# Attention with memory slots and a SwiGLU block: another order of the loads in each round, and of the first gate and value products

## The chip, the cores and the metric

The kernel runs on one core of a Trainium2 chip. The metric is device time in microseconds (us) for one execution of the whole program; lower is better. The engines are TensorE (PE, with its weight loads shown apart as PEld), VectorE (DVE), ScalarE (ACT), GpSimd (POOL) and SyncE (SP). Each engine runs its own instructions in order and waits for the others, and for transfers, through semaphores.

## The reference

```python
def _attn_ref(q, k, v, phi):            # q, k, v: [8, 8, 576, 64]; phi: [8, 8, 576, 32]
    a = np.exp(phi - max over m);  a = a / sum over m
    k_m = einsum('bhsm,bhsd->bhmd', a, k)       # 32 memory slots for each head
    v_m = einsum('bhsm,bhsd->bhmd', a, v)
    scores = q @ k_m.T / sqrt(64)
    attn = softmax over the 32 slots of scores
    return attn @ v_m

def _moe_ref(x, w_gate, w_val, w_out):  # x: [4608, 512]; 512 -> 1536 -> 512
    g = x @ w_gate
    return (g * sigmoid(g) * (x @ w_val)) @ w_out
```

The attention's output, with its heads put side by side, is `x` of the second function: 8 batches of 576 tokens with 512 features. All inputs and the output are float32; the kernel computes its products in bfloat16.

## The kernel before, in words

All 8 batches run through the same stages, on 96 partitions of 6 tokens where tokens are the contraction.

*Memory sums.* `phi_exp` (line 146) exponentiates phi. `kv_sum` (line 160) multiplies it into keys and values, 48 small matmuls for a batch, and `kv_denominators` (line 172) makes the sums that `k_norm` and `v_norm` divide by. `kv_T` transposes the result (lines 210, 214) and copies it into `t_kT` (line 216). For batches 2 to 7 `kv_items` does keys and values together, so line 160 waits for both loads. For batches 0 and 1 keys (`k_items`) and values (`v_items`) go apart.

*Queries.* For batches 0 and 1 TensorE transposes them (`q_T`). For batches 2 to 7 a DMA transpose issued on SP does it (`load_qT`, line 99: from the tile `t_q` to `t_qT`).

*Scores.* `scores` (line 287) multiplies the transposed keys with the transposed queries, `z_inv` (line 307) makes the softmax denominators, `norm` (line 316) the weights `t_A`.

*Gate and value.* The values of the memory are first multiplied into the weights: `u_round` (line 330) makes `t_U` from `t_kT` and a chunk of 512 columns of both weight matrices, three chunks a batch; `u_item` does a whole chunk, `u_both_halves` one half of it. Each of 24 slots of a batch (`gv_slot`, line 364) then multiplies `t_U` with `t_A` for gate and value. ACT applies Silu (line 380), DVE multiplies (line 387). Slots 0 to 3 need only the first half of chunk 0, slots 4 to 7 its second half, slots 8 to 15 chunk 1.

*Output.* For each pair of batches 9 tiles of 128 tokens take 12 matmuls each (line 420). A tile is copied out of PSUM (lines 430, 432) and stored by SP (line 434). These units are kept in a list, the backlog, and put between other work.

*The order of the work* is written out by hand, and each engine follows it as written. A prelude issues the loads for batches 0 to 3 and the weights; then comes the hand-written start for batches 0 and 1; then a loop with one round for each batch from 2 to 7. A round takes the scores, softmax and slots of batch `b` and, spread between the slots, the memory sums of batch `b + 1` and its transposed queries. It also issues the loads for later batches: keys and values of `b + 1`, phi and queries of `b + 2`.

*The load queue.* All loads but the first two of phi are issued by POOL, one after the other. An issue waits until its buffer is free, and what follows waits behind it. Keys and values have two buffers in turn, phi two, `t_qT` two. The query tile has two slots, given out by hand:

```python
Q_SLOT = (0, 1, 0, 0, 1, 0, 1, 0)
```

Batches 2, 3, 5 and 7 share slot 0 and batches 4 and 6 share slot 1, where batch 1 was before. So the load of batch 3's queries waits for batch 2's DMA transpose, that of batch 5 for batch 3's, that of batch 6 for batch 4's, that of batch 7 for batch 5's; that of batch 4 waits for nothing that is still running. SP issues the DMA transposes and the stores, in order too; the transpose for batch 3 stands in the middle of its round (`n = 12` of 24), the later ones at the head of the slots.

Of the kernel before, what the change touches and what calls it, by code (L numbers as in the profile page):

```python
# [14 lines left out]
def kernel(  # L15
# [21 lines left out]
    B, H, S, D = q.shape  # L37
# [34 lines left out]
    def load_k(b):  # L72
        t = inp.tile([P, 2, H, J * D], BF16, tag="kv", name="t_kv")
        nc.gpsimd.dma_start(out=t[:, 0], in_=k[b].rearrange("h (p j) d -> p h (j d)", p=P))  # L74
        kvs[b] = t

    def load_v(b):
        nc.gpsimd.dma_start(
            out=kvs[b][:, 1], in_=v[b].rearrange("h (p j) d -> p h (j d)", p=P)
        )  # L80
# [10 lines left out]
    def load_q(b):  # L91
        t = inp.tile([P, H, J * D], BF16, tag=f"q{Q_SLOT[b]}", bufs=1, name="t_q")
        nc.gpsimd.dma_start(out=t, in_=q[b].rearrange("h (p j) d -> p h (j d)", p=P))  # L93
        qs[b] = t

    def load_qT(b):

        t = att.tile([128, H, 3, P], BF16, tag="qT", name="t_qT")
        nc.sync.dma_start_transpose(
            out=t.rearrange("p h j t -> p (h j) t"),  # L100
            in_=qs[b].rearrange("p h f -> p (h f)"),
        )
        for i in range(NP):
            qTs[b, i] = t[:, 2 * i:2 * i + 2].rearrange("p h j t -> p h (j t)")
# [5 lines left out]
    def load_w(which, c, half):  # L110

        src = (moe_w_gate, moe_w_val)[which]
        if half == 0:
            W[which, c] = wpool.tile(
                [128, 2, NP, HC], BF16, tag=f"W{which}{c}", name=f"W{which}{c}"
            )
        f0 = c * CH + half * HC
        nc.gpsimd.dma_start(
            out=W[which, c][:, half],
            in_=src[:, f0:f0 + HC].rearrange("(i p) f -> p i f", p=128),  # L120
        )
# [20 lines left out]
    def phi_exp(b):  # L142
        t = att.tile([P, J, NG, NP, M], BF16, tag="ephi", name="t_ephi")
        src = phis.pop(b).rearrange("p (i g) (j m) -> p g i j m", g=NG, m=M)
        for g in range(NG):
            nc.scalar.activation(  # L146
                out=t[:, :, g].rearrange("p j i m -> p i j m"), in_=src[:, g], func=AF.Exp
            )
        ephis[b] = t
# [84 lines left out]
    def k_items(b):  # L234


        def sums():
            box["k"] = ps.tile([128, NG * D + NG], FP32, tag="b", name="p_kv")
            kv_sum(b, box["k"], (0,))

        def norm():
            kv_denominators(b, box["k"], NG * D)
            k_norm(b, box["k"][:, 0:NG * D].rearrange("p (g a d) -> p g a d", g=NG, a=1))

        return [sums, norm, lambda: kv_T(b, (0,))]

    def v_items(b):


        def sums():  # L250
            p = ps.tile([128, NG * D], FP32, tag="b", name="p_kv")
            kv_sum(b, p, (1,))
            v_norm(b, p.rearrange("p (g d) -> p g d", g=NG))

        return [sums, lambda: kv_T(b, (1,))]
# [22 lines left out]
    def gv_banks():  # L278
        return [
            ps.tile([128, CH], FP32, tag="b", name=f"p_{'gv'[r]}") for r in range(2)  # L280
        ]

    def scores(b, g):
        p = gv_banks()
        for i in range(NP):
            for r in range(2):
                nc.tensor.matmul(  # L287
                    p[r][32 * i:32 * i + 32, 0:HALF],
                    lhsT=kTs[b][64 * r:64 * r + 64, g, 32 * i:32 * i + 32],
                    rhs=qTs[b, i][64 * r:64 * r + 64, g],  # L290
                    start=True,
                    stop=True,
                    tile_position=(64 * r, 32 * i),
                )
        e = att.tile([128, 2, HALF], BF16, tag=f"E{g}", name="t_E")
        for r in range(2):
            nc.scalar.activation(out=e[:, r], in_=p[r][:, 0:HALF], func=AF.Exp, scale=sm_scale)  # L297
        es[b, g] = e
# [23 lines left out]
    def u_round(b, parts, evac):  # L322

        banks = []
        for which, c, halves in parts:
            f0, f1 = HC * halves[0], HC * (halves[-1] + 1)
            p = [ps.tile([128, CH], FP32, tag="b", name=f"p_u{g}") for g in range(NG)]
            for i in range(NP):
                for g in range(NG):
                    nc.tensor.matmul(  # L330
                        p[g][32 * i:32 * i + 32, f0:f1],
                        lhsT=kTs[b][64 * g:64 * g + 64, 2, 32 * i:32 * i + 32],
                        rhs=W[which, c][64 * g:64 * g + 64, halves[0]:halves[-1] + 1, i],
                        start=True,
                        stop=True,
                        tile_position=(64 * g, 32 * i),
                    )
            for g in range(NG):
                if (b, which, c, g) not in Us:
                    Us[b, which, c, g] = upool.tile(  # L340
                        [128, CH], BF16, tag=f"U{which}{c}{g}", name="t_U"
                    )
                banks.append((Us[b, which, c, g][:, f0:f1], p[g][:, f0:f1]))
        for (t, p), e in zip(banks, evac):
            if e == "a":
                nc.scalar.copy(out=t, in_=p)  # L346
            else:
                nc.vector.tensor_copy(out=t, in_=p)  # L348
# [105 lines left out]
    def u_item(b, c, evac="avav"):  # L454

        both = ((0, c, (0, 1)), (1, c, (0, 1)))
        return lambda: u_round(b, both, evac)

    def u_both_halves(b, c, half, evac="avav"):

        both = ((0, c, (half,)), (1, c, (half,)))
        return lambda: u_round(b, both, evac)
# [4 lines left out]
    def run(items):  # L467
        for x in items:
            x()
# [10 lines left out]
    def exp_tables():  # L480
        nc.scalar.preload_act_table_set("natural_log_exp_and_others")  # L481

    def gv_slots(b):
        return [lambda s=s: gv_slot(b, s) for s in range(2 * NJF)]

    def warm(n):

        p = po.tile([128, DM], FP32, tag="o", name="p_oo")
        for _ in range(n):
            nc.tensor.matmul(p[:, 0:128], lhsT=bones, rhs=bones, start=True, stop=True)  # L490
# [15 lines left out]
    load_v(0)  # L506
    for which in range(2):
        load_w(which, 0, 0)
    for which in range(2):
        load_w(which, 0, 1)  # L510
    load_v(1)
    for c in range(1, NCH):
        for half in range(2):
            for which in range(2):
# [17 lines left out]
    k0, k1, v0, v1 = k_items(0), k_items(1), v_items(0), v_items(1)  # L532
# [35 lines left out]
    g0, g1 = gv_slots(0), gv_slots(1)  # L568
    warm(6)
    run([u_both_halves(0, 0, 0)])  # L570
    warm(6)
    run(g0[:2])
    run([u_both_halves(0, 0, 1)] + g0[2:5] + v1[:1] + g0[5:6] + v1[1:] + g0[6:7])
    run([u_item(1, 0)] + g0[7:8] + g1[:6])
    for c in range(1, NCH):
        s = 8 * c
        run([u_item(0, c)] + g1[s - 2:s] + g0[s:s + 4])
# [5 lines left out]
    def take(n):  # L583
        nonlocal backlog
        n = max(0, min(n, len(backlog)))
        part, backlog = backlog[:n], backlog[n:]
        return part

    for b in range(2, B):
        last = b + 1 == B  # L590
        exp_tables()
        if b == 2:
            load_qT(2)
            phi_exp(2)
            run(take(28))
            run(kv_items(2)[:1] + take(6) + kv_items(2)[1:] + take(14))
        run(take(2))
        for g in range(NG):
            scores(b, g)
        if not last:  # L600
            load_k(b + 1)
            load_v(b + 1)
        if b + 2 < B:
            load_phi(b + 2, nc.gpsimd)
            load_q(b + 2)
        run(take(8))
        if not last:
            phi_exp(b + 1)
        for g in range(NG):
            z_inv(b, g)  # L610
        nc.scalar.preload_act_table_set("silu_and_others")
        run(take(14))
        norm(b, 0)
        norm(b, 1)
        if b == 2:
            run(take(4))
            run([u_item(2, 0)] + take(6) + [u_item(2, 1)])
        run(take(12))
        rest = take(len(backlog))
        g = gv_slots(b)  # L620
        streams = [(g, 0, 24), (rest, 0, 24), ([u_item(b, 2)], 5, 6)]
        if not last:
            n = 12 if b == 2 else 0
            streams += [
                ([lambda: load_qT(b + 1)], n, n),
                (kv_items(b + 1), 8, 14),
                ([u_item(b + 1, 0)], 15, 17),
                ([u_item(b + 1, 1)], 21, 23),
            ]
        spread(*streams)  # L630
        flush_mul()
        backlog += out_list(b)
# [29 lines left out]
```

## Time and profile before

| | before |
|---|---|
| time, median of 3 runs | 261.36 us (260.73 to 262.14) |
| the profiled execution: time | 263.36 us |
| the profiled execution: span | 261.4 us |
| mean granted TensorE clock over the span | 0.987 |
| PE busy | 245.3 us |
| DVE / ACT / POOL busy | 153.2 / 167.0 / 36.3 us |
| HBM read / written | 42.47 MB / 9.44 MB |
| DMA transposes on SP | 6 |

The span runs from the first to the last instruction in the profile; the time of an execution has some 2 us around it. A timeline row has the start, the duration, the engine, the line of the kernel, the operation, output and inputs, the shape, and in brackets the idle time of the engine just before with what ended it. A row of the DMA view has output and input, the issuing queue, the number of issues, the size, and the time from issue to landing. Names such as `t_kv<-in_v_dram` read "into the tile t_kv from the input v".

### The profile page before, as it was taken

Reading aid. Unit: us, or ns where it says so; the run is one execution under the profiler, and the core shown is the slowest. Engines: PE = TensorE matmul, PEld = TensorE weight load, DVE = VectorE, ACT = ScalarE, POOL = GpSimd, SP = SyncE. Lnnn points to the kernel's source line nnn. Section 1 sums busy time; section 2 is a strip of 40 time slices with the busy share of each in tenths; the row PEclk is TensorE's granted clock in tenths of the full one; section 3 lists DMA queues with packets and bytes.
Section 4 is the critical chain, followed back from the end, with each engine's and each line's share of the span. In section 5 each row is a group of like instructions: output and inputs, shape, how many; then the busy total and the mean of one; then the engine's idle time right before and its main releaser. Section 6 shows DMA issues by size and latency. Waiting matters only on the chain.

```text
span 261.4 us, 6631 instructions
## 1 busy us (share of the span) xinstructions
PE 245.3 (94%) x2626; PEld 149.3 (57%) x2626; DVE 153.2 (59%) x332; ACT 167.0 (64%) x362; POOL 36.3 (14%) x53
## 2 busy tenths in 40 slices
PE   7999799999999993599999999999999999999993
PEld 7976467675445761246654675456655665467541
DVE  0037599982256884048874667467845787477421
ACT  1469588882386574467589656966797577666300
POOL 8433453000540000300301030000000000000000
PEclk9999999999999999599999999999999999999999
DMA  7999999996999999699397969345014510220143
GB/s 184 204 203 198 200 196 205 223 227 106 169 231 259 237 158 148 73 209 291 60 201 161 196 106 219 82 118 90 0 43 119 98 40 11 82 70 3 40 120 80
DMA packets 49006, 36.99 MB, mean 141 GB/s; under 512 B 15952, under 2 KB 43600, under 8 KB 48976
## 3 DMA queue, kind: packets, MB, share of 16 engines
q0 software_dynamic: 27632, 22.42, 54.4%
q1 hardware_dynamic: 20560, 13.57, 24.3%
q10 hardware_dynamic: 784, 0.59, 0.9%
q8 instruction: 20, 0.33, 0.6%
q14 instruction: 10, 0.08, 0.1%
HBM read 42.47 MB, written 9.44 MB: 199 GB/s over the span
## 4 chain that ended last, share of the span: by engine, by line
PE 78%; DMA 19%; POOL 1%; issue 1%; DVE 0%; POOLq 0%
PE p_oo L420 36%; PE p_g L364 17%; PE p_v L364 16%; DMA t_qT<-t_q 8%; DMA t_kv<-in_v_dram 6%; DMA t_kv<-in_k_dram 5%; PE p_u L330 4%; PE p_kv L160 2%; PE p_g L287 1%; PE p_kv L172 1%; PE p_v L307 1%; PE p_g L307 1%; POOL t_q L86 0%; POOL t_kv L74 0%; DVE t_o L432 0%
## 5 line engine op out<-in xcount | busy, mean ns | idle before, releaser
L420 PE MATMUL p_oo<-WO,t_h 128*128 128x512 bf16 x432 | 114.8, 384 | 0.0
L380 ACT ACTIVATE t_sg<-p_g 128x288 bf16<-128x288 f32 x192 | 77.0, 415 | 41.7 <-PE p_g L364 34.5
L387 DVE TENSOR_TENSOR t_h<-t_sg,p_v 128x288 bf16<-128x288 bf16 x192 | 84.0, 452 | 22.2 <-PE p_v L364 18.7
L364 PEld LDWEIGHTS <-t_U 128*128 128x128 bf16 x768 | 72.7, 98 | 35.1 <-issue 7.3
L364 PE MATMUL p_g<-t_A,t_U 128*128 128x288 bf16 x384 | 78.5, 286 | 0.3 <-ACT t_U L346 0.3
L364 PE MATMUL p_v<-t_A,t_U 128*128 128x288 bf16 x384 | 77.6, 286 | 0.0
L420 PEld LDWEIGHTS <-t_h 128*128 128x128 bf16 x432 | 41.8, 99 | 41.0 <-issue 4.5
L432 DVE COPY t_o<-p_oo 128x512 f32<-128x512 f32 x28 | 19.3, 691 | 56.2 <-PE p_oo L420 56.1
L348 DVE CAST t_U<-p_u 128x512 bf16<-128x512 f32 (+1 forms) x50 | 31.0, 662 | 0.8
L346 ACT CAST t_U<-p_u 128x512 bf16<-128x512 f32 (+1 forms) x50 | 26.1, 572 | 6.5 <-PE p_u L330 6.4
L490 PE MATMUL p_oo<-bones 128*128 128x128 bf16 x218 | 16.0, 235 | 1.5 <-DVE bones L502 1.5
L430 ACT COPY t_o<-p_oo 128x512 f32<-128x512 f32 x8 | 4.7, 591 | 19.3 <-PE p_oo L420 19.1
L93 POOL DMA_DIRECT2D t_q<-in_q_dram x6 | 4.6, 773 | 87.0 <-DMA t_qT<-t_q 86.2
L330 PE MATMUL p_u<-W,t_kT 64*32 64x512 bf16 (+1 forms) x400 | 15.7, 373 | 0.3 <-DVE t_kT L216 0.2
L490 PEld LDWEIGHTS <-bones 128*128 128x128 bf16 x218 | 14.3, 106 | 2.3 <-DVE bones L502 1.5
L146 ACT ACTIVATE t_ephi<-t_phi 96x768 bf16<-96x768 f32 x16 | 12.5, 843 | 4.3 <-DMA t_phi<-in_phi_dram 4.3
L287 PE MATMUL p_g<-t_qT,t_kT 64*32 64x288 bf16 x64 | 5.2, 307 | 7.6 <-DMA t_qT<-t_q 7.2
L180 DVE RECIPROCAL t_rS<-p_kv 128x2 f32<-128x2 f32 x8 | 1.4, 171 | 18.1 <-PE p_kv L172 18.1
L316 DVE TENSOR_TENSOR t_A<-t_E,t_lz 128x576 bf16<-128x576 bf16 x16 | 11.5, 751 | 0.4 <-ACT t_lz L311 0.4
L297 ACT ACTIVATE t_E<-p_g 128x288 bf16<-128x288 f32 x16 | 6.6, 412 | 8.0 <-PE p_v L287 7.8
L311 ACT ACTIVATE t_lz<-t_lz 128x576 f32<-128x576 f32 x16 | 10.9, 683 | 0.5
L481 ACT ACT_TABLE_LOAD x7 | 9.0, 1283 | 1.3 <-PEq L646 1.2
(42 smaller groups left out, 128.0 us busy)
## 6 DMA issues: line engine op xcount, KB each, us to landing
t_kv<-in_k_dram POOLq DMA_DIRECT2D x8, 576.0 KB, 11.3
t_kv<-in_v_dram POOLq DMA_DIRECT2D x8, 576.0 KB, 15.4
out_dram<-t_o SPq DMA_DIRECT2D x24, 192.0 KB, 2.5
t_phi<-in_phi_dram POOLq DMA_DIRECT2D x6, 576.0 KB, 16.5
t_q<-in_q_dram POOLq DMA_DIRECT2D x6, 576.0 KB, 7.5
out_dram<-t_o SPq DMA_DIRECT2D x24, 128.0 KB, 2.4
W<-in_moe_w_gate_dram POOLq DMA_DIRECT2D x6, 256.0 KB, 13.0
W<-in_moe_w_val_dram POOLq DMA_DIRECT2D x6, 256.0 KB, 12.9
```

Of the source, the lines that this page charges most:

```text
L146: nc.scalar.activation(out=t[:, :, g].rearrange("p j i m -> p i j m"), in_=src[:, g], func=AF.Exp)
L311: nc.scalar.activation(out=lz, in_=lz, func=AF.Exp, scale=-1.0)
L316: nc.vector.tensor_tensor(out=a, in0=es.pop((b, g)), in1=lzs.pop((b, g)), op=ALU.mult)
L330: nc.tensor.matmul(p[g][32 * i:32 * i + 32, f0:f1], lhsT=kTs[b][64 * g:64 * g + 64, 2, 32 * i:32 * i + 32], rhs=W[which, c][64 * g:64 * g ...
L346: nc.scalar.copy(out=t, in_=p)
L348: nc.vector.tensor_copy(out=t, in_=p)
L364: nc.tensor.matmul(p[:, 0:HALF], lhsT=Us[b, which, c, g][:, 128 * o:128 * (o + 1)], rhs=atts[b, g][:, r], start=(g == 0), stop=(g == NG - 1),)
L380: nc.scalar.activation(out=sg, in_=gate, func=AF.Silu)
L387: nc.vector.tensor_tensor(out=dst, in0=sg, in1=val, op=ALU.mult)
L420: nc.tensor.matmul(mine["p"], lhsT=hts[c, jf][:, 128 * u:128 * (u + 1)], rhs=WO[jf], start=(jf == 0), stop=(jf == NJF - 1),)
L432: nc.vector.tensor_copy(out=t_o, in_=mine["p"])
L490: nc.tensor.matmul(p[:, 0:128], lhsT=bones, rhs=bones, start=True, stop=True)
```

## The change

There are two edits. In each round of the loop from batch 2, the load of the queries of `b + 2` is issued first, ahead of keys and values of `b + 1` and phi of `b + 2`; before, it came last of the four. In the start, the load of the values of batch 1 goes ahead of the weights' second half of chunk 0 (gate and value), and the first gate and value work is put in another order: the memory sums of batch 1's values come after three slots of batch 0, and batch 1's product with chunk 0, which was one whole round of line 330 (`u_item(1, 0)`), becomes two rounds of a half (`u_both_halves(1, 0, 0)` and `(1, 0, 1)`), the first of them ahead of batch 0's second half. By the end of this stretch the slots done are the same.

```diff
@@ prelude @@
     load_v(0)
     for which in range(2):
         load_w(which, 0, 0)
+    load_v(1)
     for which in range(2):
         load_w(which, 0, 1)
-    load_v(1)
     for c in range(1, NCH):
...
@@ start, batches 0 and 1 @@
     run([u_both_halves(0, 0, 0)])
     warm(6)
-    run(g0[:2])
-    run([u_both_halves(0, 0, 1)] + g0[2:5] + v1[:1] + g0[5:6] + v1[1:] + g0[6:7])
-    run([u_item(1, 0)] + g0[7:8] + g1[:6])
+    run(g0[:3] + v1[:1] + g0[3:4] + v1[1:])
+    run([u_both_halves(1, 0, 0)] + g1[:3])
+    run([u_both_halves(0, 0, 1)] + g1[3:4] + g0[4:7])
+    run([u_both_halves(1, 0, 1)] + g0[7:8] + g1[4:6])
     for c in range(1, NCH):
...
@@ a round of the loop @@
         for g in range(NG):
             scores(b, g)
+        if b + 2 < B:
+            load_q(b + 2)
         if not last:
             load_k(b + 1)
             load_v(b + 1)
         if b + 2 < B:
             load_phi(b + 2, nc.gpsimd)
-            load_q(b + 2)
         run(take(8))
```

## The prediction

> **What bounds the kernel now.** I read the page first: how busy TensorE (PE) is, and at which clock.
>
> ```profile
> PE 245.3 (94%) x2626; PEld 149.3 (57%) x2626; DVE 153.2 (59%) x332; ACT 167.0 (64%) x362; POOL 36.3 (14%) x53
> PEclk9999999999999999599999999999999999999999
> ```
>
> PE is busy for 245.3 of 261.4 us, and every slice but one has the full clock. So time can only come out of PE's holes and the one slow slice, the seventeenth (104.6 to 111.1 us). Next, PE's timeline, at the two holes and at places to compare them with (start, duration, and in brackets the idle time before with what ended it):
>
> ```profile
> 31.53 0.56 PE L160 MATMUL p_kv<-t_kv,t_ephi 96*32 96x64 bf16 x48 [1.61 <-DMA t_kv<-in_v_dram]
> 33.43 0.62 PE L330 MATMUL p_u<-W,t_kT 64*32 64x512 bf16 x16 [0.20 <-DVE t_kT L216]
> ...
> 69.66 0.29 PE L287 MATMUL p_g<-t_qT,t_kT 64*32 64x288 bf16 x1
> ...
> 71.77 0.29 PE L307 MATMUL p_g<-t_E,bones 128*128 128x288 bf16 x1
> ...
> 88.05 0.85 PE L160 MATMUL p_kv<-t_kv,t_ephi 96*32 96x128 bf16 x48
> ...
> 99.47 0.59 PE L420 MATMUL p_oo<-WO,t_h 128*128 128x512 bf16 x2
> 107.28 0.42 PE L287 MATMUL p_g<-t_qT,t_kT 64*32 64x288 bf16 x1 [7.21 <-DMA t_qT<-t_q]
> ...
> 111.28 0.33 PE L307 MATMUL p_g<-t_E,bones 128*128 128x288 bf16 x1
> ```
>
> The large hole is 7.21 us ahead of the scores of batch 3 (line 287), which wait for that batch's transposed queries. It has a second price. From the first score to the first matmul of the denominators (line 307), batch 2 takes 71.77 - 69.66 = 2.11 us, batch 3 takes 111.28 - 107.28 = 4.00 us for the same work: 1.89 us more. The windows view says why (the granted clock stands ahead of the last two columns):
>
> ```profile
> 103.00:104.00 1.00, 0.00 (x0) 0.00 (x0) 0.00 (x0) 0.00 (x0) 0.00 (x0) 1.00 1.58 127
> 104.00:105.00 1.00, 0.00 (x0) 0.00 (x0) 0.00 (x0) 0.00 (x0) 0.00 (x0) 0.76 1.14 67
> ...
> 109.20:111.30 2.10, 2.10 (x7) 0.73 (x6) 0.00 (x0) 1.35 (x2) 1.35 (x3) 0.50 0.98 115
> ```
>
> PE fell idle at 99.47 + 0.59 = 100.06; the clock was still whole at 104, dropped at about 104.5, 4.4 us into the idle time, and was at a half until work had gone on for some 4 us. The hole costs 7.21 + 1.89 = 9.10 us. The small hole is 1.61 + 0.20 us at the values of batch 1.
>
> Why is the transpose late? The issues on the load queue (POOL), on SP, and the time from issue to landing (DMA view, asked for each issue):
>
> ```profile
> 16.71 0.79 POOL L78 DMA_DIRECT2D t_kv<-in_v_dram  x1 [1.96 <-DMA t_kv<-in_k_dram]
> ...
> 68.49 0.77 POOL L93 DMA_DIRECT2D t_q<-in_q_dram  x1 [25.27 <-DMA t_qT<-t_q]
> 69.25 0.77 POOL L74 DMA_DIRECT2D t_kv<-in_k_dram  x1
> 70.01 0.77 POOL L78 DMA_DIRECT2D t_kv<-in_v_dram  x1
> 70.77 0.79 POOL L69 DMA_DIRECT2D t_phi<-in_phi_dram  x1
> 71.54 0.78 POOL L93 DMA_DIRECT2D t_q<-in_q_dram  x1
> 72.30 0.78 POOL L74 DMA_DIRECT2D t_kv<-in_k_dram  x1
> 73.06 0.78 POOL L78 DMA_DIRECT2D t_kv<-in_v_dram  x1
> 73.82 0.80 POOL L69 DMA_DIRECT2D t_phi<-in_phi_dram  x1
> 107.79 0.77 POOL L93 DMA_DIRECT2D t_q<-in_q_dram  x1 [33.17 <-DMA t_qT<-t_q]
> ```
>
> ```profile
> 85.04 8.54 SPq L99 DMA_TRANSPOSE t_qT<-t_q  x1
> ...
> 119.24 4.45 SPq L99 DMA_TRANSPOSE t_qT<-t_q  x1
> ```
>
> ```profile
> t_kv<-in_v_dram POOLq DMA_DIRECT2D x1, 576.0 KB, 14.8
> ...
> t_q<-in_q_dram POOLq DMA_DIRECT2D x1, 576.0 KB, 8.8
> t_kv<-in_k_dram POOLq DMA_DIRECT2D x1, 576.0 KB, 13.0
> t_kv<-in_v_dram POOLq DMA_DIRECT2D x1, 576.0 KB, 16.1
> t_phi<-in_phi_dram POOLq DMA_DIRECT2D x1, 576.0 KB, 17.0
> t_q<-in_q_dram POOLq DMA_DIRECT2D x1, 576.0 KB, 21.2
> t_kv<-in_k_dram POOLq DMA_DIRECT2D x1, 576.0 KB, 24.5
> t_kv<-in_v_dram POOLq DMA_DIRECT2D x1, 576.0 KB, 31.9
> t_phi<-in_phi_dram POOLq DMA_DIRECT2D x1, 576.0 KB, 32.9
> ...
> t_qT<-t_q SPq DMA_TRANSPOSE x1, 4.9
> t_qT<-t_q SPq DMA_TRANSPOSE x1, 22.2
> ...
> t_kv<-in_v_dram POOLq DMA_DIRECT2D x1, 576.0 KB, 11.5
> ```
>
> From 68.49 eight loads go out in one burst. Issue plus time to landing gives, in the queue's order: q3 at 77.3, k3 at 82.25, v3 at 86.1, phi4 at 87.8, q4 at 92.7, k4 at 96.8, v4 at 105.0, phi5 at 106.7 (the digit is the batch). They land strictly in order. Batch 3's transpose, issued at 85.04, shares the DMA engines with five of them, takes 22.2 us where batch 2's took 4.9 with the queue empty, and lands at 107.24, half a microsecond after the last load. What happens meanwhile, from the DMA view of 90 to 92 us (q0 carries the loads, q1 the transpose; packets, MB, share):
>
> ```profile
> q0 software_dynamic: 358, 0.27, 111.8%
> q1 hardware_dynamic: 361, 0.09, 53.1%
> ```
>
> Load and transpose alternate packet by packet. So what matters for the transpose is how long the loads go on, not how many bytes it has itself.
>
> **The change, part by part.**
>
> *Queries first in each round.* No instruction is added. After q3 the queue now issues q4, k3, v3, phi4, then q5. Batch 5's queries go into the buffer that batch 3's transpose reads, so q5 stands until that transpose has landed, and k4, v4 and phi5 stand behind it. They used to slip in ahead of q5; that is the 33.17 us of idle time at 107.79, which came after them.
>
> (a) The gain. The last load ahead of the waiting q5 is phi4. The five loads q3, q4, k3, v3, phi4 are the same bytes as the five that had landed by 92.7, so phi4 lands then. If the transpose, issued at about 85 as now, got nothing until then and took its 4.9 us afterwards, it would be there by 97.6; it has a share from 85 on, so I expect 95 to 97. The scores of batch 3 need it 100.06 - 88.05 = 12.01 us after PE starts the sums of keys and values of batch 3, which is not before 100. The 7.21 us hole goes, and with it the 1.89 us: -9.10.
>
> (b) The price. q4 now lands where k3 did (82.25), k3 where v3 did (86.1), and v3 after that, where it was phi4 and then q4. PE begins the sums of batch 3 at 88.05, and v3's slack against that was 88.05 - 86.1 = 1.95 us; this is the cover that is used up. When does v3 land? At the latest with the fifth load of before, 92.7; at the earliest with the fourth, 87.8 (but phi4 added only 1.7 us to the queue, and each of the others 3.9 to 4.95). The row nearest to it is q4's: the same bytes, beside the same transpose, 92.7 - 87.8 = 4.9 us after its predecessor. So 86.1 + 4.9 = 91.0. PE then waits 91.0 - 88.05 = 2.95 us at line 160: +2.95, with ends at 0 and +4.65.
>
> (c) The clock. Does this new hole cost clock as the old one did? The 1.61 us hole near 30 us left the clock alone (a 9 in the fifth slice of its row); the 7.21 us hole lost it 4.4 us in. 2.95 lies nearer to the short one and short of 4.4, so I take 0; the other end is the +1.89 of the old hole. The Trainium skill (TensorE: Matmul & The Clock Gate, Part 1) says that the gate looks at free-running windows of 3.4 us and halves the clock after an idle one. By that rule 2.95 us never holds a whole idle window, and the sum stays the same; a hole between 3.4 and 6.8 us would lose the clock by chance, which makes it a little more of a risk than the 4.4 seen here; this trace has no hole between 1.61 and 7.21 us to show it.
>
> (d) What waits behind q5. q5 goes out about 0.55 us after the transpose lands (107.24 to 107.79 now), so by 98.2 at the latest. v5's row from the next round, which stood third behind a query load, took 11.5 us from its issue, which is two issues of 0.77 after the query's. So v4 is there by 98.2 + 1.5 + 11.5 = 111.2. The sums of batch 4, in the chain of waits:
>
> ```profile
> 123.98 0.78 PE p_kv L160 x48
> ```
>
> stand at 123.98 now and move to 117.8 with the gain below. 6.6 us of cover; if the transpose were later than that, each microsecond would be lost on PE. phi4 (92.7 instead of 87.8) is exponentiated only after the scores of batch 3, at 103, and phi5 a batch later. In the later rounds the transpose stands at the head of its round (119.24 now, when the round's first scores were at 107.28), half a round earlier than batch 3's, so what stands behind q6 and q7 has more room, and the transposes now find an empty queue. No PE hole is there to be won. POOL issues the same DMAs; k, v and phi go out one issue (0.77 us) later, which the transfers ahead of them hide.
>
> *Values of batch 1 ahead of two weight halves, and the order of the first gate and value matmuls.* v1 (issued 16.71, landed 31.5) goes past two loads of weights on POOL; the three together are the same bytes, so the weights' second half lands by 31.5 instead. The order on PE puts the first-half work of both batches ahead of it. One round of 16 matmuls on line 330 becomes two half-width rounds: at most one more round of 0.62 us with its copies. At best both waits go: -1.81; at worst they stay and the round is added: +0.62. I take 0 for the sum, and it need not be known: the chain of loads (the same bytes up to q2, then batch 2's transpose, then q3) sets v3's landing, and PE, early or late by this much, meets it there. An earlier PE only waits longer.
>
> *Sum.* -9.10 + 2.95 + 0 + 0 = -6.15 us on this execution, whose span is 261.4 and whose time is 263.36, 2.0 more outside the span and 2.0 over the median of the three runs. Taken off the median: 261.36 - 6.15 = 255.2 us.
>
> **The rivals.**
>
> 1. *No new wait.* If v3 lands by 88.05 (the end of 87.8 in b), all of the 9.10 is kept: 252.3. For it: phi4 and v3 were only 1.7 us apart, so the queue's engines run ahead of the landings. Against: q4 took 4.9 just there. 0.12.
>
> 2. *The new hole is long enough to lose the clock.* v3 at 92.7, or a startup that brings PE 1.5 us earlier: 4.65 + 1.89 of the 9.10 are given back, 258.8. For it: the transpose now takes every second packet from 85 on. Against: batch 3's values stand ahead of phi4 in the queue, and q4's row already holds this sharing. 0.14.
>
> 3. *Slower: the wait for the values takes the place of the wait for the queries and outgrows it.* v4 landed 105.0 - 96.8 = 8.2 us after k4 while the transpose ran. If k3 and v3 both went at that pace behind q4, v3 would land at 82.25 + 16.4 = 98.65, PE would wait 10.6 and lose 1.89: 264.8. It decides at a landing of 88.05 + 9.10 - 1.89 = 95.3. Against: k3 has nearly landed when the transpose begins at 85. 0.06.
>
> 4. *The change doesn't do what it says.* If the transpose is starved by what is left (k3, v3, phi4) and by the stores, and lands after 107 still, nothing is won: 261.4 or a little more. Against: the 4.9 us of batch 2 with the queue empty; it has to be 10 us late. 0.05.
>
> **How the numbers follow.** The forecast has the rest, 0.63: 255.2. The range takes in rivals 1 and 2 with a little of the startup's gain, 252.0 to 259.0, and leaves out 3 and 4, 0.11. About 0.5% (1.3 us) is what a measurement of this kernel can tell from no change: forecast and rivals 1 and 2 lie below 260.05, 0.89, of which I give 0.01 to the middle for a startup that goes wrong. Faster 0.88, same 0.06, slower 0.06.
>
> **What would show it.** Right: the transpose of batch 3 lands some 10 to 12 us after its issue and the 7.21 us ahead of line 287 is gone; every 9 in the clock's row; a new wait of about 3 us at line 160 for the values of batch 3, near 88 us; on POOL a wait before q5 that ends when that transpose lands, at 95 to 97, with k4, v4, phi5 behind it; the hole at 31 us smaller, and PE no further on by 88 us than it is worth. Wrong: no wait at line 160 (rival 1), a clock below 1 after it (rival 2), or a wait there beyond 7 us (rival 3); a wait that stays at line 287 (rival 4); a wait for k4 or v4 near 118 us, which would say that (d) has less cover than I give it.

## The result and the profile after

| | before | after |
|---|---|---|
| median of 4 runs each | 261.69 us (260.73 to 262.14) | 254.82 us (254.38 to 255.31) |
| ratio, 95% interval | | 0.9743 [0.9708, 0.9778] |
| profiled execution: time / span | 263.36 / 261.4 us | 254.38 / 252.3 us |
| mean granted TensorE clock | 0.987 | 0.997 |

The change makes the kernel faster by 6.9 us; 6.15 were forecast. The two profiled executions stand 9.0 us apart, more than the medians; the first experiment asks why. The page, first TensorE and its clock in 40 slices:

```profile
PE 243.2 (96%) x2642; PEld 148.9 (59%) x2642; DVE 153.5 (61%) x334; ACT 167.0 (66%) x364; POOL 36.3 (14%) x53
PEclk9999999999999999999999999999999999999998
```

The 5 in the clock's row is gone. TensorE's timeline at the places shown of before:

```profile
28.28 0.56 PE L160 MATMUL p_kv<-t_kv,t_ephi 96*32 96x64 bf16 x48 [0.17 <-DMA t_kv<-in_v_dram]
...
30.18 0.41 PE L330 MATMUL p_u<-W,t_kT 64*32 64x256 bf16 x16 [0.69 <-DVE t_kT L216]
30.98 0.42 PE L364 MATMUL p_g<-t_A,t_U 128*128 128x288 bf16 x2 [0.38 <-ACT t_U L346]
...
88.05 0.85 PE L160 MATMUL p_kv<-t_kv,t_ephi 96*32 96x128 bf16 x48 [0.49 <-DMA t_kv<-in_v_dram]
...
100.00 0.29 PE L287 MATMUL p_g<-t_qT,t_kT 64*32 64x288 bf16 x1
...
102.11 0.29 PE L307 MATMUL p_g<-t_E,bones 128*128 128x288 bf16 x1
```

There is no idle time ahead of line 287, and from the scores to line 307 it takes 2.11 us as for batch 2. The new wait for v3 is there, but it is 0.49 us. The load queue, SP, and times to landing:

```profile
68.67 1.53 POOL L93 DMA_DIRECT2D t_q<-in_q_dram  x2 [25.45 <-DMA t_qT<-t_q]
70.20 0.77 POOL L74 DMA_DIRECT2D t_kv<-in_k_dram  x1
70.96 0.77 POOL L78 DMA_DIRECT2D t_kv<-in_v_dram  x1
71.72 0.79 POOL L69 DMA_DIRECT2D t_phi<-in_phi_dram  x1
94.75 0.77 POOL L93 DMA_DIRECT2D t_q<-in_q_dram  x1 [22.24 <-DMA t_qT<-t_q]
95.51 0.77 POOL L74 DMA_DIRECT2D t_kv<-in_k_dram  x1
96.27 0.77 POOL L78 DMA_DIRECT2D t_kv<-in_v_dram  x1
```

```profile
84.48 6.95 SPq L99 DMA_TRANSPOSE t_qT<-t_q  x1
```

```profile
t_kv<-in_k_dram POOLq DMA_DIRECT2D x1, 576.0 KB, 13.8
t_kv<-in_v_dram POOLq DMA_DIRECT2D x1, 576.0 KB, 17.0
t_phi<-in_phi_dram POOLq DMA_DIRECT2D x1, 576.0 KB, 19.8
t_qT<-t_q SPq DMA_TRANSPOSE x1, 9.7
...
t_kv<-in_v_dram POOLq DMA_DIRECT2D x1, 576.0 KB, 11.3
```

q3, q4, k3, v3 and phi4 go out; then q5 stands for 22.24 us until batch 3's transpose has landed, at 84.48 + 9.7 = 94.2. The transpose took 9.7 us, not 22.2. k3 landed at 84.0, v3 at 87.96, phi4 at 91.5, and v4, let go later, at 96.27 + 11.3 = 107.6.

Of the runs of the experiments below, one of e1, one of e2 and two of e4, each over 1.5% above the fastest of its kernel, are left out of the ratios but not of the medians.

### The profile page after: what moved, and what is told of

Read it like the earlier page. It is cut to its first block, busy times and chain, and to the rows that moved or that the text cites. A ratio compares the mean times of both kernels' runs of the same rounds, so it can differ in the third digit from the quotient of the medians.

```text
span 252.3 us, 6668 instructions
## 1 busy us (share of the span) xinstructions
PE 243.2 (96%) x2642; PEld 148.9 (59%) x2642; DVE 153.5 (61%) x334; ACT 167.0 (66%) x364; POOL 36.3 (14%) x53
## 3 DMA queue, kind: packets, MB, share of 16 engines
q1 hardware_dynamic: 20560, 13.57, 22.7%
## 4 chain that ended last, share of the span: by engine, by line
PE 68%; DMA 27%; POOL 1%; issue 1%; DVE 1%; ACT 0%; POOLq 0%; SPq 0%
PE p_oo L420 29%; PE p_g L364 15%; PE p_v L364 15%; DMA t_kv<-in_v_dram 13%; DMA t_q<-in_q_dram 12%; PE p_u L330 4%; DMA t_qT<-t_q 2%; PE p_kv L160 2%; PE p_kv L172 1%; PE p_g L287 1%; POOL t_kv L74 1%; PE p_v L307 1%; PE p_g L307 1%; POOL t_q L93 0%; POOL t_phi L69 0%
## 5 line engine op out<-in xcount | busy, mean ns | idle before, releaser
L420 PE MATMUL p_oo<-WO,t_h 128*128 128x512 bf16 x432 | 113.1, 379 | 0.0
L330 PEld LDWEIGHTS <-t_kT 64*32 64x32 bf16 x416 | 4.3, 89 | 8.3 <-issue 6.6
L160 PE MATMUL p_kv<-t_kv,t_ephi 96*32 96x128 bf16 (+1 forms) x480 | 7.3, 210 | 0.7 <-DMA t_kv<-in_v_dram 0.7
```

Of the source, the lines that this page charges most:

```text
L160: nc.tensor.matmul(p[32 * i:32 * i + 32, n * g:n * (g + 1)], lhsT=ephis[b][:, j, g, i], rhs=kvs[b][:, w0:w1, 2 * i + g, j * D:(j + 1) * D] ...
L330: nc.tensor.matmul(p[g][32 * i:32 * i + 32, f0:f1], lhsT=kTs[b][64 * g:64 * g + 64, 2, 32 * i:32 * i + 32], rhs=W[which, c][64 * g:64 * g ...
L420: nc.tensor.matmul(mine["p"], lhsT=hts[c, jf][:, 128 * u:128 * (u + 1)], rhs=WO[jf], start=(jf == 0), stop=(jf == NJF - 1),)
```

## The experiments

Medians, and ratios to the kernel before with their 95% intervals. The kernels of one set (the expectations say "call") ran on one chip, beside the kernel before, which had medians of 261.72, 262.14 and 262.07 us in the three sets.

| kernel | set | us | ratio |
|---|---|---|---|
| e1 before, again | 1 | 261.71 | 0.9984 [0.9954, 1.0014] |
| e2 loop's loads alone | 1 | 255.27 | 0.9747 [0.9702, 0.9792] |
| e3 start alone | 1 | 261.99 | 1.0011 [0.9985, 1.0037] |
| e4 own query slot, no wait | 1 | 263.09 | 1.0024 [0.9985, 1.0062] |
| e5 keys, values, queries, phi | 2 | 258.17 | 0.9847 [0.9800, 0.9894] |
| e6 mixed order | 2 | 253.84 | 0.9683 [0.9641, 0.9726] |
| e7 queries, phi, keys, values | 2 | 260.31 | 0.9917 [0.9882, 0.9952] |
| e8 after, again | 2 | 254.98 | 0.9731 [0.9691, 0.9770] |
| e9 mixed order, old start | 3 | 253.60 | 0.9678 [0.9644, 0.9711] |
| e10 mixed order, again | 3 | 254.05 | 0.9697 [0.9662, 0.9731] |
| e11 e5 with the hole filled | 3 | 257.07 | 0.9810 [0.9759, 0.9860] |

**Was the profile of before typical?** e1 is the kernel before, unchanged.

> The kernel before, once more. Its profiled execution took 263.36 us and lost 9.10 us at the scores of batch 3; its other runs have medians of 261.4 to 261.7, and the change moved those by 6.9 us while the two profiled executions stand 9.0 apart. Theory A: the hole differs from run to run, and 263.36 was a run with a long one; then this profile shows a hole at line 287 shorter than 7.21 us (about 5 us, with part of the slow clock) if its time is near 261.5. Theory B: the hole is the same in all runs and the profiled execution was long elsewhere; then the hole is 7 us again, and the missing 2 us lie outside the span or spread over it. Time 261.4 either way.

Its profiled execution took 261.77 us, close to the median. TensorE's timeline:

```profile
105.19 0.42 PE L287 MATMUL p_g<-t_qT,t_kT 64*32 64x288 bf16 x1 [5.44 <-DMA t_qT<-t_q]
...
109.19 0.45 PE L307 MATMUL p_g<-t_E,bones 128*128 128x288 bf16 x1
```

The hole is 5.44 us, and the work after it takes 4.00 us where 2.1 are normal. The clock was still at a half after line 307 (windows view, the granted clock third from the end):

```profile
109.00:110.00 1.00, 1.00 (x5) 0.54 (x4) 0.00 (x0) 0.32 (x2) 0.54 (x1) 0.50 1.32 204
```

From line 307 to the sums of batch 4 it took 122.34 - 109.19 = 13.15 us, where the changed kernel takes 114.70 - 102.11 = 12.59. So this run, close to the median, loses 5.44 + 1.90 + 0.56 = 7.90 us here; the execution profiled first lost 9.10. Theory A holds.

**Which half of the change?** e2 keeps the edit in the loop alone, e3 the two in the prelude and the start.

```diff
# e2, against before                  # e3, against after
+        if b + 2 < B:                -        if b + 2 < B:
+            load_q(b + 2)            -            load_q(b + 2)
         if not last:                          if not last:
...
         load_phi(b + 2, nc.gpsimd)            load_phi(b + 2, nc.gpsimd)
-            load_q(b + 2)            +            load_q(b + 2)
```

> Only the new order of the loads in the loop; the start is that of before. Theory A (the wait of batch 5's queries keeps k4, v4 and phi5 away from the transpose, and the start is worth next to nothing): the transpose of batch 3 lands 9 to 11 us after its issue, no hole at line 287, line 160 starts at about 88 for batch 3 as v3 lands then; time 254.5 to 255.5, ratio 0.973 to 0.978. Theory B (the start gives part of the 6.9 us): time 256 to 257.5.

> Only the new start; the loop's loads are in the order of before. Theory A: PE is 0.6 us earlier at the sums of batch 2 (62.99 instead of 63.55) and gives it back at the scores of batch 3, which wait for the transpose as before; time as before within 0.5 us, ratio 0.998 to 1.002, the hole at line 287 longer by about 0.6. Theory B: the 0.6 us or more stay; ratio 0.995 to 0.997.

The loop's loads alone give 0.9747, the start alone 1.0011. In e2 the sums of batch 3 waited 1.24 us for v3:

```profile
88.74 0.85 PE L160 MATMUL p_kv<-t_kv,t_ephi 96*32 96x128 bf16 x48 [1.24 <-DMA t_kv<-in_v_dram]
```

In e3 TensorE was at the sums of batch 2 0.5 us earlier than in e1 (62.74; e1 63.23) and then stood at line 287 for longer (5.81; e1 5.44):

```profile
62.74 0.85 PE L160 MATMUL p_kv<-t_kv,t_ephi 96*32 96x128 bf16 x48
...
105.07 0.42 PE L287 MATMUL p_g<-t_qT,t_kT 64*32 64x288 bf16 x1 [5.81 <-DMA t_qT<-t_q]
```

**Is it the wait or the order?** e4 keeps the change's order and takes the reason to wait away.

```diff
-    Q_SLOT = (0, 1, 0, 0, 1, 0, 1, 0)
+    Q_SLOT = (0, 1, 0, 0, 1, 2, 1, 2)
```

> The changed kernel with one edit: batches 5 and 7 have a third query slot, so that the queries of batch 5 wait for no transpose; the order of the loads is that of the change. Theory A (the wait is what matters): q5, k4 and v4 follow phi4 in one burst, the transpose of batch 3 shares the engines with them and lands at 103 to 107, the hole at line 287 is back with 3 to 7 us and some of the slow clock; time 258 to 262. Theory B (the order matters, since q4 is out of the way early): no hole, 254.8.

The whole gain is gone. POOL runs on (q5, k4, v4 from 72.44), and TensorE now has both waits:

```profile
72.44 0.77 POOL L93 DMA_DIRECT2D t_q<-in_q_dram  x1
73.20 0.77 POOL L74 DMA_DIRECT2D t_kv<-in_k_dram  x1
73.96 0.77 POOL L78 DMA_DIRECT2D t_kv<-in_v_dram  x1
```

```profile
89.35 0.85 PE L160 MATMUL p_kv<-t_kv,t_ephi 96*32 96x128 bf16 x48 [1.89 <-DMA t_kv<-in_v_dram]
...
107.11 0.39 PE L287 MATMUL p_g<-t_qT,t_kT 64*32 64x288 bf16 x1 [4.24 <-DMA t_qT<-t_q]
```

So the wait makes the gain; the order alone only adds the wait for v3. Its transpose took 22.7 us.

**How much may stand ahead of the wait?** In e5 k4 and v4 go out before the waiting q5; in e7 phi4 goes ahead of k3 and v3.

```diff
# each round, after: q(b+2), k(b+1), v(b+1), phi(b+2)
# e5:                k(b+1), v(b+1), q(b+2), phi(b+2)
# e7:                q(b+2), phi(b+2), k(b+1), v(b+1)
```

> The changed kernel with another order in each round: keys, values, queries, phi. The queries of batch 5 still wait for batch 3's transpose, but k4 and v4 now stand ahead of them and go out in the first burst; only phi5 is held back. Theory A (the time of the transpose is set by the loads ahead of the waiting q5): seven loads go on to about 100 us instead of five to 91, the transpose lands at about 101 to 104, the hole at line 287 is 1 to 4 us, and line 160 for batch 3 has no wait; time 256 to 260. Theory B (any wait of the queue is enough, since the transpose gets going): no hole, 254.5.

> The changed kernel with queries and phi both ahead of keys and values (q3, q4, phi4, k3, v3). v3 now lands in the fifth place, where the changed kernel has phi4 at 90.4 to 91.5. Theory A (landings go by place in the queue, and what comes after 88 us shares with the transpose): line 160 for batch 3 starts at 91 to 92.5, a hole of 3.5 to 5 us; if the clock holds, 3 to 4 us over the changed kernel, 258 to 259; if it drops after this hole as it did after 7.21 us, up to 1.9 more. Theory B (a later v3 is hidden): 255.

e5 lies where theory A put it: the transpose took 17.6 us and landed at 102.4, and the hole is 2.60 us. In e7 v3 landed at 92.9, and the hole of 5.09 us at line 160 lost the clock too: 5.3 us over the changed kernel of the same set, where 3 to 4 were expected with the clock whole and up to 1.9 more without it. Timelines of e5, then e7:

```profile
102.48 0.42 PE L287 MATMUL p_g<-t_qT,t_kT 64*32 64x288 bf16 x1 [2.60 <-DMA t_qT<-t_q]
```

```profile
92.91 1.47 PE L160 MATMUL p_kv<-t_kv,t_ephi 96*32 96x128 bf16 x48 [5.09 <-DMA t_kv<-in_v_dram]
```

**Can the wait for v3 be had for nothing?** e6 is the changed kernel with k3 and v3 ahead of q4, in the round of batch 2 alone; e8 is the changed kernel beside it.

```diff
-        if b + 2 < B:
+        if b + 2 < B and b > 2:
             load_q(b + 2)
...
         if b + 2 < B:
+            if b == 2:
+                load_q(b + 2)
             load_phi(b + 2, nc.gpsimd)
```

> The changed kernel, but in the round of batch 2 alone keys and values of batch 3 go ahead of the queries of batch 4 (q3, k3, v3, q4, phi4, then q5 first as in the change). Theory A (the wait at line 160 for v3 is the price of the new order, 0.5 to 1.2 us in two profiles): v3 lands at 84 to 86, no wait at line 160, the transpose as in the changed kernel; 0.5 to 1.2 us less than the changed kernel in the same call. Theory B (that wait is slack that something else takes up): the same time as the changed kernel.

> The changed kernel once more, beside the others of this call: 254.8, ratio 0.972 to 0.977, the wait at line 160 for batch 3 between 0.3 and 1.5 us, the transpose of batch 3 landing 9 to 11 us after its issue.

e6 is 1.1 us faster than e8, and their runs don't overlap (253.49 to 254.57; 254.62 to 255.74). e8 waited a little longer for v3 than I had expected at most; e6 doesn't wait. First e8, then e6:

```profile
89.46 0.85 PE L160 MATMUL p_kv<-t_kv,t_ephi 96*32 96x128 bf16 x48 [1.67 <-DMA t_kv<-in_v_dram]
```

```profile
88.32 0.85 PE L160 MATMUL p_kv<-t_kv,t_ephi 96*32 96x128 bf16 x48
```

**What is the new start worth, with nothing behind it to hide it?** e9 is e6 with the start of before, e10 is e6 once more.

> The loads as in the mixed order (keys and values of batch 3 ahead of the queries of batch 4, queries first from the next round on), with the start of the kernel before. With v3 early, nothing downstream should hide what the start is worth. Theory A (the new start brings PE about 0.5 us forward, as four profiles show at the sums of batch 2: 62.7 to 63.35 against 63.2 to 63.55): 0.3 to 0.6 us over the mixed kernel of the same call, 254.2 to 254.5. Theory B (the new start is worth nothing: the lost wait is spent on the extra half round): the same time, 253.8.

> The mixed kernel once more, beside the one with the old start: 253.8, ratio 0.966 to 0.972, no wait at line 160 for batch 3 and none at line 287.

Theory A fell. The old start gives 253.60 (253.48 to 253.89), the new one 254.05 (253.78 to 254.58): worth nothing, if not a loss of 0.4 us. In e10 the copies that follow at once on the first rounds take what the wait for v1 gave back:

```profile
30.49 0.41 PE L330 MATMUL p_u<-W,t_kT 64*32 64x256 bf16 x16 [0.69 <-DVE t_kT L216]
31.29 0.42 PE L364 MATMUL p_g<-t_A,t_U 128*128 128x288 bf16 x2 [0.38 <-ACT t_U L346]
```

In e9 the wait for v1 was only 0.45 us, since TensorE came later to it (30.59 us; e1 29.73):

```profile
31.04 0.55 PE L160 MATMUL p_kv<-t_kv,t_ephi 96*32 96x64 bf16 x48 [0.45 <-DMA t_kv<-in_v_dram]
```

e9 has the lowest median found. The changed kernel did not run beside it; their ratios to before are 0.9678 and, in e8, 0.9731, with intervals that overlap.

**Is the slow clock a price of its own?** e11 is e5 with idle work in the hole.

```diff
         run(take(2))
+        if b == 3:
+            warm(45)
         for g in range(NG):
             scores(b, g)
```

> The order keys, values, queries, phi again (258.17; its hole of 2.60 us at line 287 was followed by 3.5 us at half clock where 2.1 are normal), with 45 idle-time matmuls of 128 columns on TensorE ahead of the scores of batch 3, which fill about 2.5 us of that hole and compute nothing that is used. Theory A (the slow stretch after the hole is a price of its own, paid because TensorE stood still for 2.6 us): the clock stays whole, the scores start where they did, and 1.4 us come back: 256.6 to 257.0. Theory B (the clock fell for another reason, such as where its window stood): the clock falls as before and the time is 258.2 or more.

257.07 us, 1.1 us less than e5, in another set (their ratios to before are 0.9810 and 0.9847, with intervals that overlap). The clock's row shows the mechanism without that doubt. Windows view, the granted clock third from the end; e5, then e11:

```profile
101.50:102.00 0.50, 0.00 (x0) 0.00 (x0) 0.00 (x0) 0.00 (x0) 0.00 (x0) 1.00 1.26 280
102.00:102.50 0.50, 0.02 (x7) 0.03 (x8) 0.00 (x0) 0.00 (x0) 0.00 (x0) 0.60 0.72 270
102.50:104.00 1.50, 1.17 (x18) 0.49 (x20) 0.00 (x0) 1.02 (x4) 1.01 (x2) 0.50 0.00 1
```

```profile
102.00:103.00 1.00, 0.86 (x25) 0.53 (x23) 0.00 (x0) 0.20 (x1) 0.07 (x1) 1.00 0.28 105
103.00:104.00 1.00, 0.99 (x5) 0.49 (x5) 0.00 (x0) 1.00 (x5) 1.00 (x2) 1.00 0.00 0
```

## Why the prediction was right, and where it was not

The time came out 0.4 us from the forecast, and the mechanism was the one forecast; but two terms of the sum were off and made up for each other. That they did so nearly to the full is luck; both were read from the one execution profiled before, a long one.

**(a) The gain.** The hole at line 287 and the slow stretch went as said, because the waiting q5 keeps k4, v4 and phi5 off the transpose; e4 shows that it is this wait. I put the landing at 95 to 97; it came at 94.2. The size is another matter. The 9.10 us were right for the execution they were read from, and that was a long one: e1, near the median, loses 7.90. The step that failed is the last one of the sum, taking a difference read from an execution of 263.36 off a median of 261.36: of the 1.6 us between that execution and e1 (261.77), 1.2 lay in the very hole that went and its slow clock.

**(b) The price.** 2.95 us were forecast; 0.49, 1.24, 1.67 and 1.89 were measured (after, e2, e8, e4). v3 landed at 87.96, not at 91.0, close to the end I had set at 87.8, and at 89.3 in e8. The failed step is the landing in the sum, 86.1 + 4.9, and both of its numbers were too large. k3, which was to land at 86.1, landed at 84.0 (84.9 in e2, 85.3 in e4, 85.5 in e8), and v3 came 3.96 us after it (3.8 to 3.9 in those three). The two numbers are again rows of the one long execution. In e1, the same kernel, v3, phi4 and q4 were issued at 69.83, 70.59 and 71.36 us, with these times to landing:

```profile
t_kv<-in_v_dram POOLq DMA_DIRECT2D x1, 576.0 KB, 14.3
t_phi<-in_phi_dram POOLq DMA_DIRECT2D x1, 576.0 KB, 15.9
t_q<-in_q_dram POOLq DMA_DIRECT2D x1, 576.0 KB, 18.9
```

So v3 landed at 84.1, phi4 at 86.5, and q4 at 90.3, 3.8 us after its predecessor. The same sum from these rows gives 84.1 + 3.8 = 87.9, a wait of 0.2 us for a TensorE that is there at 87.73, a little under the four that were measured. So the step by places in the queue holds, and its sizes were those of one execution. It is not phi4's place ahead of q4 that made the 4.9 us. With phi4 ahead, q4 came 3.8 us after it in e1 and e3; straight behind v3 it came 3.8 to 5.3 us after that (e5, e6, e9, e10, e11). Why landings differ so from one execution to the next stays open.

On the profiled pair alone rival 1 (no new wait, 252.3) would have seemed the better forecast: the spans are 9.1 us apart. Against e1, which took 261.77 us, the account closes: 7.90 for the hole and its clock, less 0.49 for v3, is 7.41, and the two executions are 261.77 - 254.38 = 7.39 apart. With the waits of e2 and e8 it would be 6.2 to 6.7; the medians moved by 6.9.

**(c) The clock.** Nothing was lost, as taken; but the reason given doesn't hold. I called 2.95 us safe, since it was nearer to 1.61 and short of 4.4. e5 lost the clock in a hole of 2.60, and e4 in one of 1.89, so my forecast hole might well have cost 1.4 us more, as e5's did (106.01 - 102.48 = 3.53 us from the first score to line 307, where 2.11 are normal). That it was 0.49 saved the term. The Trainium skill's rule (TensorE: Matmul & The Clock Gate, Part 1), a whole idle window of 3.4 us, would have let both of those holes pass; these runs say otherwise.

**(d) What waits behind q5.** Right: q5 went out 0.57 us after the transpose landed, v4 was there at 107.6 (111.2 at the latest by my sum), and no wait for k4 or v4 shows.

**The start.** I put 0 in the sum, because PE would meet v3 anyway. The changed kernel and e2 differ by the start alone and bear that out (0.9743, 0.9731 in e8; e2 0.9747); in e3 (1.0011) it is the transpose that PE meets. e10 against e9 goes further: the start is worth nothing even with v3 out of the way.

**The rivals.** Rival 2's mechanism is real in another order: in e7 v3 landed at 92.9, the wait for it grew to 5.09 us, the clock fell, and 5.3 us of the gain went. Rivals 3 and 4 did not come up. What a transpose that stays late costs, e5 shows in part, with two more loads ahead of the wait, and e4 in full, with no wait.

## What to carry to other kernels

The transpose came later the longer a queue of bulk loads ran beside it (9.7, 17.6 and 22.7 us in after, e5 and e4), so look for a wait that already exists, such as a buffer still being read, and put the loads that aren't urgent behind it; then place the urgent ones ahead (e9: 253.60). What of this the order does and what the wait does is told apart by giving the waiting load a buffer of its own. And before a gain read from one profiled execution is taken off a median, see how long the same hole is in a second one.

## What the runs showed of the hardware that I had not expected

The clock can fall after a hole much shorter than the one seen first, and after work has resumed. In e4 TensorE was idle from 87.46 to 89.35 us, 1.89 us; windows view:

```profile
89.00:90.00 1.00, 0.65 (x48) 0.68 (x48) 0.00 (x0) 0.00 (x0) 0.00 (x0) 1.00 1.15 219
90.00:91.00 1.00, 1.00 (x31) 0.72 (x20) 0.31 (x2) 0.00 (x0) 0.00 (x0) 0.55 1.30 193
91.00:92.00 1.00, 0.78 (x4) 0.52 (x4) 0.78 (x3) 0.41 (x1) 0.00 (x0) 0.50 1.43 127
```

It had the full clock until about 90.1 and half of it from there, 0.7 us after it was at work again. In e8 a hole of 1.67 us at the same place cost nothing. From the beginning of the hole to the fall it took 4.4 us in the first profile of before, 2.6 in e4 and 2.2 in e5: no fixed time after the hole begins.

A DMA transpose that takes 4.9 us with the queue empty took 9.7, 17.6 and 22.7 us with fewer and more loads beside it (after, e5, e4), landing within 3 us of the last of them: 2.7 us after it, 0.6 after it, and 1.2 ahead of it.
